# Moving the packs-times-W_in tiles to another place within 256 bytes

## The chip, the core and the metric

The kernel runs on one core of one Trainium2 chip. The metric is the device time of one execution in microseconds (us), taken as the median of several runs. Beside the runs stands one execution recorded by the hardware profiler; all rows shown below come from it.

## The reference

Two attentions in a row, and a feed-forward network behind them, all in float32:

```python
p_packed = sm_attn(p, k, v)              # 32 packed queries per head read all 576 tokens
out = sm_attn(q, p_packed, p_packed)     # 576 tokens read the 32 packed rows
x = out.transpose(0, 2, 1, 3).reshape(B * S, H * D)      # 4608 tokens x 512
h = x @ w_in                             # w_in is 512 x 2048
g = h * (1.0 / (1.0 + np.exp(-h)))
return (g @ w_out).astype(np.float32)    # w_out is 2048 x 512
```

There are 8 batches, 8 heads of 64 elements, 576 tokens and 32 packs in each batch.

## The kernel before

The second attention is a sum over packs, so the kernel never forms x. For each batch it multiplies the 32 packed rows of each head by the part of W_in that belongs to that head (line 310). The result, with two heads in turn for each partition, is the tile that is changed here: for one quarter of the 2048 hidden columns it holds 2 x 512 columns. `Packs.upper` (line 587) copies it from PSUM into `pw_hi`, rounded to the shorter float type (float32r) with which TensorE multiplies, and `Packs.lower` (line 590) writes what the rounding left over into `pw_lo`. The shares of the second attention (the softmax of the tokens over the packs) are split in the same way into `a2_hi` and `a2_lo` (lines 551 and 555).

`h_products` (line 622) then makes h for 288 tokens (half a batch) and 128 hidden columns out of six matmuls: for each of two parities upper x upper, upper x lower, lower x upper. The pack tile is the stationary operand, 128 x 128 of it loaded by one LDWEIGHTS for each matmul, and 288 columns of shares are the moving operand. `h_products` runs 32 times for the first two batches with both halves in one call, and 96 times for the other six, with two blocks of 128 hidden columns in one call: 128 calls of twelve matmuls, 1536 in all.

ScalarE applies the activation, GpSimd makes sums of it, ScalarE and VectorE split the result into `g_hi` and `g_lo` (lines 685 and 689), and line 695 multiplies it by W_out: `g` is stationary, and 256 columns of `wo_hi`, `wo_lo` or of sums of them (`sums_of_w`) are moving. In the first two batches these matmuls have 512 moving columns. A list written out by hand (`ORDER`) fixes the order of all steps. On TensorE a stretch of 12 or 24 matmuls of line 622 is followed by one of 21 or 42 of line 695, and so on, with smaller steps of the attention between them (lines 310, 414 and 433).

The code sets where operands begin within 256 bytes. All large tiles start at a multiple of 256 bytes. The shares begin `AT_A` = 20 floats, 80 bytes, into their tile. A small tile of `AT_G` = 16 floats (64 bytes) is allocated ahead of `gp_main`, so that `g`, `g_hi` and `g_lo` of the later six batches begin at 64. `wo_hi`, `wo_lo`, `sums_of_w` and the pack tiles begin at 0. Rows of all of these step in multiples of 256 bytes. So a stationary block of packs lies (0 - 80) mod 256 = 176 bytes past the place of its moving shares, and a stationary block of `g` lies 64 past that of its moving weights (0 past it in the first two batches).

The pack tiles have two pools: `pw` for all packs of the first two batches and for the first two quarters of the others, `pw_b` for the last two quarters of the others. Each name takes two tiles in turn. `edge` is a pool at the right end of the memory that holds one tile of `EDGE` floats, of which 128 are used (line 423); the tiles right of the middle lie against it.

Of the kernel before, what the change touches and what calls it, by code (L numbers as in the profile page):

```python
# [10 lines left out]
F32R = mybir.dt.float32r  # L11
# [8 lines left out]
P = 128  # L20
# [11 lines left out]
JW = DFF // NJ  # L32
# [93 lines left out]
"""  # L126

TP_BUFS = 4
EDGE = 504
AT_G = 16  # L130
AT_A = 20
A_PART = 320
ON_TOKENS = (0,)
SCALE = 1.0 / math.sqrt(D)
# [6 lines left out]
def packed_attention_ffn(ctx: ExitStack, tc: tile.TileContext, pkT, qT, v, w_in, w_out, out):  # L141
# [17 lines left out]
    pw = ent(tc.tile_pool(name="pw", bufs=2))  # L159
# [35 lines left out]
    made = {}  # L195
# [3 lines left out]
    def in_turn(pool, shape, dtype, name, bufs=2):  # L199
        n = turns[id(pool), name] = turns.get((id(pool), name), -1) + 1  # L200
        return pool.tile(shape, dtype, name=name, tag=f"{name}_{n % bufs}", bufs=1)
# [43 lines left out]
    class Weights:  # L245
# [51 lines left out]
        def upper(self, n):  # L297
            hi, _ = self.both(n)
            nc.scalar.copy(hi, self.raw[n][1].bitcast(F32))
# [15 lines left out]
    class Attention:  # L315
# [106 lines left out]
        def scaled1(self):  # L422
            self.pp = edge.tile([P, EDGE], F32, name="pp")[:, :P]
            nc.vector.tensor_tensor(
                self.pp.rearrange("p (r d) -> p r d", r=2),
                self.ps[:, : 2 * D].rearrange("p (r d) -> p r d", r=2),
                self.rd.rearrange("p (r o) -> p r o", o=1).broadcast_to([P, 2, D]),
                ALU.mult,
            )
# [112 lines left out]
        def upper2(self, hf):  # L542
            if (self.b, hf) == (EARLY - 1, 1):
                both = [a2x.tile([P, 2, A_PART], F32R, name=name) for name in ("a2_hi", "a2_lo")]
            else:
                both = [in_turn(a2p, [P, 2, A_PART], F32R, name, 3) for name in ("a2_hi", "a2_lo")]
            hi, lo = (t[:, :, AT_A : AT_A + HS] for t in both)
            made["a2", self.b, hf] = hi, lo
# [8 lines left out]
    class Packs:  # L557
# [21 lines left out]
        def upper(self):  # L579
            b, j = self.b, self.f // FJ  # L580
            if self.f % FJ == 0:
                pool = pw_b if b >= EARLY and j >= 2 else pw
                both = [in_turn(pool, [P, 2 * JW], F32R, name) for name in ("pw_hi", "pw_lo")]
                made["pw", b, j] = [t.rearrange("p (r n) -> p r n", r=2) for t in both]
            c = slice(self.f % FJ * P, (self.f % FJ + self.nf) * P)
            self.hi, self.lo = (t[:, :, c] for t in made["pw", b, j])
            nc.scalar.copy(self.hi, self.ps)
# [426 lines left out]
```

## Time and profile before

| what | value |
|---|---|
| median of 3 runs | 675.63 us (675.42 to 675.71) |
| the profiled execution's own time | 674.6 us |
| its span, first to last instruction | 672.8 us |
| TensorE busy | 655.4 us, 97% |
| VectorE, ScalarE, GpSimd busy | 66%, 65%, 36% |
| granted TensorE clock | 1.00 of full speed |

The span is what the trace shows; 1.8 us of the profiled execution lie around it. Matmuls are pipelined: the duration of one in the trace is longer than the step from one to the next, so a rate is read from the distance between starts, or from the length of a stretch divided by its number of matmuls.

### The profile page before, as it was taken

Reading aid. Unit: us, or ns where it says so; the run is one execution under the profiler, and the core shown is the slowest. Engines: PE = TensorE matmul, PEld = TensorE weight load, DVE = VectorE, ACT = ScalarE, POOL = GpSimd, SP = SyncE. Lnnn points to the kernel's source line nnn. Section 1 sums busy time; section 2 is a strip of 40 time slices with the busy share of each in tenths; the row PEclk is TensorE's granted clock in tenths of the full one; section 3 lists DMA queues with packets and bytes.
Section 4 is the critical chain, followed back from the end, with each engine's and each line's share of the span. In section 5 each row is a group of like instructions: output and inputs, shape, how many; then the busy total and the mean of one; then the engine's idle time right before and its main releaser. Section 6 shows DMA issues by size and latency. Waiting matters only on the chain.

```text
span 672.8 us, 15186 instructions
## 1 busy us (share of the span) xinstructions
PE 655.4 (97%) x6130; PEld 588.5 (87%) x6130; DVE 442.2 (66%) x618; ACT 435.5 (65%) x732; POOL 245.0 (36%) x361
## 2 busy tenths in 40 slices
PE   8889999999999999999999999999999999999997
PEld 6666787888868989999989999989899999989996
DVE  4999999987755457745675535773748554654375
ACT  4797997764656547654865645676676658646652
POOL 1101214343304434344476343425363343444400
PEclk9999999999999999999999999999999999999999
DMA  9748674858879597785846738783788677470614
GB/s 358 331 158 335 221 270 150 297 208 302 328 293 361 165 374 266 288 276 172 310 158 269 304 84 323 282 348 116 255 321 326 236 240 297 156 284 30 219 48 142
DMA packets 55077, 166.60 MB, mean 248 GB/s; under 512 B 21472, under 2 KB 26592, under 8 KB 47328
## 3 DMA queue, kind: packets, MB, share of 16 engines
q1 hardware_dynamic: 55008, 165.63, 67.1%
q8 instruction: 49, 0.80, 0.5%
q14 instruction: 20, 0.16, 0.1%
HBM read 134.74 MB, written 26.74 MB: 240 GB/s over the span
## 4 chain that ended last, share of the span: by engine, by line
PE 72%; DVE 11%; DMA 6%; ACT 5%; issue 4%; POOL 1%; SPq 1%; DVEq 0%; ACTq 0%; POOLq 0%
PE ps_acc L695 42%; PE ps_two L622 24%; PE ps_two L310 5%; DMA win<-in_w_out 2%; DMA sums_of_w<-sums_of_w 2%; DVE g_lo L689 2%; DVE o L853 1%; ACT g_hi L685 1%; DVE g_lo L640 1%; DMA w_quarter<-w_in 1%; DVE w_raw L279 1%; PE ps_two L414 1%; DVE pw_lo L590 1%; PE ps_two L695 1%; DVE win L291 1%
## 5 line engine op out<-in xcount | busy, mean ns | idle before, releaser
L689 DVE TENSOR_TENSOR g_lo<-g,g_hi 128x896 fp32r<-128x896 f32 x112 | 126.6, 1136 | 121.8 <-ACT g_hi L685 118.5
L695 PE MATMUL ps_acc<-wo_hi,g_hi 128*128 128x256 f32 (+1 forms) x556 | 170.0, 306 | 0.1
L695 PE MATMUL ps_acc<-wo_hi,g_lo 128*128 128x256 f32 (+1 forms) x556 | 169.3, 305 | 0.7 <-DVE g_lo L689 0.4
L695 PE MATMUL ps_acc<-wo_lo,g_hi 128*128 128x256 f32 (+1 forms) x556 | 168.7, 303 | 0.0
L622 PE MATMUL ps_two<-a_hi,pw_hi 128*128 128x288 f32 x512 | 151.8, 296 | 2.9 <-DVE pw_lo L590 1.7
L685 ACT CAST g_hi<-g 128x896 fp32r<-128x896 f32 x112 | 104.3, 935 | 74.5 <-POOL g L657 44.1
L622 PE MATMUL ps_two<-a_lo,pw_hi 128*128 128x288 f32 x512 | 150.8, 295 | 0.2 <-DVE a_lo L555 0.2
L622 PE MATMUL ps_two<-a_hi,pw_lo 128*128 128x288 f32 x512 | 150.8, 294 | 0.0
L655 POOL TENSOR_TENSOR g<-g 128x128 f32<-128x128 f32 x104 | 54.2, 521 | 250.7 <-ACT g L644 243.2
L695 PE MATMUL ps_acc<-sums_of_w,g_hi 128*128 128x256 f32 x632 | 126.3, 281 | 0.2 <-DMA sums_of_w<-sums_of_w 0.2
L695 PEld LDWEIGHTS ps_acc<-wo_hi,g_hi 128*128 128x128 f32 x556 | 104.5, 188 | 8.8 <-issue 4.4
L695 PEld LDWEIGHTS ps_acc<-wo_hi,g_lo 128*128 128x128 f32 x556 | 104.6, 188 | 7.8 <-DVE g_lo L640 2.1
L695 PEld LDWEIGHTS ps_acc<-sums_of_w,g_hi 128*128 128x128 f32 x632 | 96.5, 188 | 14.4 <-issue 10.1
L695 PEld LDWEIGHTS ps_acc<-wo_lo,g_hi 128*128 128x128 f32 x556 | 104.4, 188 | 3.9
L622 PEld LDWEIGHTS ps_two<-a_hi,pw_hi 128*128 128x128 f32 x512 | 96.6, 189 | 9.4 <-DVE pw_lo L590 3.0
L622 PEld LDWEIGHTS ps_two<-a_lo,pw_hi 128*128 128x128 f32 x512 | 96.3, 188 | 1.4 <-DVE a_lo L555 0.6
L622 PEld LDWEIGHTS ps_two<-a_hi,pw_lo 128*128 128x128 f32 x512 | 96.0, 188 | 0.2 <-DVE pw_lo L590 0.2
L695 PE MATMUL ps_acc<-sums_of_w,g_lo 128*128 128x256 f32 x316 | 87.7, 278 | 0.0
L656 POOL TENSOR_TENSOR g<-g 128x256 f32<-128x256 f32 x104 | 81.2, 782 | 6.6
L644 ACT ACTIVATE g<-ps_two 128x512 f32<-128x512 f32 x96 | 56.7, 599 | 40.2 <-PE ps_two L622 20.0
L657 POOL TENSOR_TENSOR g<-g 128x128 f32<-128x128 f32 x104 | 64.2, 618 | 6.6
L695 PEld LDWEIGHTS ps_acc<-sums_of_w,g_lo 128*128 128x128 f32 x316 | 59.4, 188 | 0.2 <-DVE g_lo L689 0.2
(145 smaller groups left out, 893.5 us busy)
## 6 DMA issues: line engine op xcount, KB each, us to landing
sums_of_w<-sums_of_w SPq DMA_DIRECT2D x74, 768.0 KB, 5.8
w_quarter<-w_in SPq DMA_DIRECT2D x22, 1024.0 KB, 8.0
kvq_t<-in_v SPq DMA_DIRECT2D x8, 1280.0 KB, 9.1
kvq_t<-in_pkT SPq DMA_DIRECT2D x7, 1216.0 KB, 8.1
out<-o SPq DMA_DIRECT2D x16, 512.0 KB, 3.1
kvq_t<-in_qT SPq DMA_DIRECT2D x7, 1152.0 KB, 8.4
w_raw<-in_w_in SPq DMA_DIRECT2D x6, 1024.0 KB, 6.9
sums_of_w<-w_sums SPq DMA_DIRECT2D x8, 768.0 KB, 3.7
```

Source lines behind the costliest of these rows:

```text
L279: nc.vector.scalar_tensor_tensor(low, up, -(2**31), low, op0=ALU.bitwise_and, op1=ALU.bitwise_or)
L291: (nc.gpsimd if n in ON_POOL else nc.vector).tensor_tensor(z, z, self.raw[n][0], ALU.add)
L310: nc.tensor.matmul(bank(par)[NP * i : NP * i + NP], lhs(r, i), rhs(r, i), start=True, stop=True)
L414: nc.tensor.matmul(self.ps[NP * i : NP * i + NP, par * D : par * D + D], e, vs[:, c, h * D : h * D + D], start=(c == 0), stop=(c == 4),)
L622: nc.tensor.matmul(bank, p[:, par, cols], a[:, par], start=(n == 0), stop=(n == len(todo) - 1))
L644: nc.scalar.activation(g[:, : 4 * P].rearrange("p (e s) -> p e s", e=2), made["h", u, None][..., :MAIN], AF.Silu)
L655: engine.tensor_tensor(x[:, 4], x[:, 0], x[:, 2], ALU.subtract)
L656: engine.tensor_tensor(x[:, 5:7], x[:, 0:5:4], one, ALU.subtract)
L657: engine.tensor_tensor(x[:, 7], x[:, 3], x[:, 6], ALU.add)
L685: nc.scalar.copy(both[0], g)
L689: nc.vector.tensor_tensor(g_lo, g, g_hi.bitcast(F32), ALU.subtract)
L695: nc.tensor.matmul(out, g[:, rows], w, start=(first and n == 0), stop=(last and n == 2), skip_group_check=True)
```

## The change

`pw_hi` and `pw_lo` become the two halves of one tile, `pw_both`. It has 64 floats more than the two together, and its content begins `AT_PW` = 14 floats (56 bytes) into it. The blocks of packs so begin at 56 within 256 bytes, which is (56 - 80) mod 256 = 232 past the place of the shares. The `edge` tile shrinks from 504 to 184 floats to make room. No instruction is added or removed, and the order stays.

```diff
-EDGE = 504
+EDGE = 184
 AT_G = 16
 AT_A = 20
+AT_PW = 14
...
             if self.f % FJ == 0:
                 pool = pw_b if b >= EARLY and j >= 2 else pw
-                both = [in_turn(pool, [P, 2 * JW], F32R, name) for name in ("pw_hi", "pw_lo")]
-                made["pw", b, j] = [t.rearrange("p (r n) -> p r n", r=2) for t in both]
+                both = in_turn(pool, [P, 4 * JW + 64], F32R, "pw_both")[:, AT_PW : AT_PW + 4 * JW]
+                made["pw", b, j] = both.rearrange("p (n r x) -> n p r x", n=2, r=2)
```

Each of the four tiles grows by 256 bytes, and `edge` gives back 1280. Tiles on the left that come after `pw` move by 512 bytes, those after `pw_b` (`g`, `g_hi`, `g_lo`) by 1024, and those on the right by 1280. All these are multiples of 256, so only the packs change their place within 256 bytes.

## Rows read from the trace of the kernel before

**Rows 1.** The page: span, busy time of TensorE, its granted clock in 40 slices.
```profile
span 672.8 us, 15186 instructions
PE 655.4 (97%) x6130; PEld 588.5 (87%) x6130; DVE 442.2 (66%) x618; ACT 435.5 (65%) x732; POOL 245.0 (36%) x361
...
PEclk9999999999999999999999999999999999999999
```

**Rows 2.** The page: the chain that ended last, shares by engine and line.
```profile
PE 72%; DVE 11%; DMA 6%; ACT 5%; issue 4%; POOL 1%; SPq 1%; DVEq 0%; ACTq 0%; POOLq 0%
PE ps_acc L695 42%; PE ps_two L622 24%; PE ps_two L310 5%; DMA win<-in_w_out 2%; DMA sums_of_w<-sums_of_w 2%; DVE g_lo L689 2%; DVE o L853 1%; ACT g_hi L685 1%; DVE g_lo L640 1%; DMA w_quarter<-w_in 1%; DVE w_raw L279 1%; PE ps_two L414 1%; DVE pw_lo L590 1%; PE ps_two L695 1%; DVE win L291 1%
```

**Rows 3.** Busy time by stretch; first figures: span of stretch, PE, PEld.
```profile
30.00:120.00 90.00, 84.85 (x659) 65.29 (x644) 85.88 (x124) 76.32 (x127) 20.02 (x15) 1.00 0.60 216
...
400.00:500.00 100.00, 99.82 (x1051) 93.28 (x1050) 59.94 (x84) 64.17 (x104) 43.49 (x66) 1.00 0.71 266
```

**Rows 4.** The chain in order of time, 500 to 560: start, length, matmuls.
```profile
507.19 3.16 PE ps_two L622 x24
510.35 2.38 PE ps_acc L695 x21
512.73 1.13 PE ps_two L310 x32
513.86 2.67 PE ps_acc L695 x21
516.53 1.58 PE ps_two L622 x12
518.11 2.38 PE ps_acc L695 x21
...
536.11 1.57 PE ps_two L622 x12
537.68 4.76 PE ps_acc L695 x42
```

**Rows 5.** The same view, 120 to 140, where line 695 has 512 columns.
```profile
127.97 2.73 PE ps_acc L695 x12
```

**Rows 6.** TensorE in order of time behind line 310: start, duration.
```profile
441.36 0.28 PE L695 MATMUL ps_acc<-sums_of_w,g_lo 128*128 128x256 f32 x1
...
442.54 0.28 PE L695 MATMUL ps_acc<-wo_hi,g_hi 128*128 128x256 f32 x1
```

**Rows 7.** The same view where line 695 follows line 622.
```profile
301.60 0.29 PE L622 MATMUL ps_two<-a_lo,pw_hi 128*128 128x288 f32 x1
301.73 0.29 PE L622 MATMUL ps_two<-a_hi,pw_lo 128*128 128x288 f32 x1
301.86 0.39 PE L695 MATMUL ps_acc<-sums_of_w,g_hi 128*128 128x256 f32 x2
```

**Rows 8.** The page: groups of line 622, busy, mean ns, idle before and releaser.
```profile
L622 PE MATMUL ps_two<-a_hi,pw_hi 128*128 128x288 f32 x512 | 151.8, 296 | 2.9 <-DVE pw_lo L590 1.7
...
L622 PEld LDWEIGHTS ps_two<-a_hi,pw_hi 128*128 128x128 f32 x512 | 96.6, 189 | 9.4 <-DVE pw_lo L590 3.0
...
L622 PEld LDWEIGHTS ps_two<-a_hi,pw_lo 128*128 128x128 f32 x512 | 96.0, 188 | 0.2 <-DVE pw_lo L590 0.2
```

**Rows 9.** Line 587 by itself: what its engine waited for (us, times).
```profile
  PE ps_two L310: 16.2, 15
```

**Rows 10.** Durations (min/median/max ns) of the writers that split tiles.
```profile
L587 ACT CAST pw_hi<-ps_two x35: 375/1016/1086, 18.0 to 591.8; 128x1024 fp32r<-128x1024 f32 x31, 128x256 fp32r<-128x256 f32 x4
...
L551 ACT CAST a_hi<-tm x14: 665/675/725, 71.0 to 605.6; 128x576 fp32r<-128x576 f32 x14
```

**Rows 11.** Who waited for whom: TensorE on the pack tiles.
```profile
PEld ps_two L622 <- DVE pw_lo L590: 3.2, 4, 2.3
...
PE ps_two L622 <- DVE pw_lo L590: 1.7, 2, 1.4
```

**Rows 12.** Instructions of line 695 from 205.4 on: stretch, PE busy.
```profile
205.40:673.00 467.60, 286.84 (x2358) 277.20 (x2358) 1.00 0.65 236
```

## The prediction

> **What bounds the kernel now.** I read the page first. TensorE is busy for 655.4 of 672.8 us, at the full clock in every slice, which is the upper of its two levels, 2.4 GHz [rows 1]. The chain that ended last is 72% TensorE; line 695 has 42% of the span, line 622 has 24%, no other line over 5% [rows 2]. Busy time by stretch says where that holds: between 400 and 500 us TensorE is busy 99.8%, in the early part (30 to 120) 94% [rows 3]. So the kernel ends when TensorE has worked through its list, and what counts is the step from one matmul to the next.
>
> That step is read from the chain in order of time, where TensorE's stretches stand with their lengths [rows 4]. Line 622 takes 3.16 us for 24 matmuls, 1.58 or 1.57 us for 12: 131 to 132 ns each, and 131.0 is what I use. At 2.4 GHz 288 columns need 288 / 2.4 = 120 ns, so 11.0 ns of each step is not streaming. Line 695 has two rhythms for the same instruction. Mostly 21 take 2.38 us and 42 take 4.76, 113.3 ns each, which is 6.6 over its 256 / 2.4 = 106.7. Behind line 310 a stretch of 21 takes 2.67 us. That is not the first wait alone: the single starts of such a stretch go from 441.36 to 442.54 in ten steps, 118.0 ns each, 11.3 over [rows 6]. With 512 columns twelve take 2.73 us, 227.5 each, 14.2 over 213.3 [rows 5]. So the excess in the short rhythm is near one sixteenth of the columns (6.6 of 106.7, 14.2 of 213.3); the long rhythm of line 695 adds some 4.5 ns. Line 622 at 11.0 has the excess of the long rhythm, in every stretch of these rows. Its own sixteenth would be 7.5 ns, a step of 127.5.
>
> **The change part by part.** *No instruction comes or goes.* The same 1536 loads and matmuls of line 622 read the packs from another place.
>
> *The new place under the loads.* This is the whole of the possible gain, and the trace of before has no stretch with packs at 56. Bounds of the step: from below 120.0, pure streaming at the granted clock; from above the long rhythm of line 695 carried over, 118.0 / 106.7 x 120 = 132.7. Within these I take the short rhythm, 127.5. The reason: the same kind of instruction is seen in both rhythms at one and the same relation (64 bytes, line 695), the relation of 0 with 512 columns is short too [rows 5], and only the relation of 176 is always long; 232 lies 24 bytes from 0 and 56 from 176. That is nearness, not proof, and it gets less than half the chance. The gain is 3.5 ns x 1536 = 5.4 us of TensorE time.
>
> *What of it reaches the end.* Line 622 takes 131.0 x 1536 = 201 us of TensorE, and the chain holds 24% of 672.8 = 161 us of it [rows 2]: 0.8. In the later stretches TensorE has nearly no idle time [rows 3], which speaks for 1.0. I take 0.9, so 4.8 us.
>
> *One tile in place of two, reading.* If a matmul now waits for the whole tile, the first upper product waits for VectorE's lower part too, which it could have done without for two steps. It does so already: of the time in which a load of line 622 waited for `pw_lo`, 3.0 us stand at the load of `pw_hi` and 0.2 at that of `pw_lo` [rows 8]; all such waits are 3.2 + 1.7 us in six places [rows 11]. Cost 0, at most 6 x 0.26 = 1.6 us if these six had been caused by something else.
>
> *One tile in place of two, writing.* ScalarE's write of the next upper part now has to wait until the old lower part is read as well, one matmul later (0.13 us). Line 587 never waited for matmuls of line 622; all its 16.2 us are for the products of line 310 [rows 9]. Cost 0. What hides it is the slack of the second tile in turn; without that it would be 35 x 0.13 = 4.6 us.
>
> *Writing at 56.* The copies of 1024 elements take 1.02 us at place 0, or 0.99 ns per element; shares, written at 80, take 675 / 576 = 1.17 [rows 10]. If the new place brought line 587 to 1.17, it would be 35 x 0.18 = 6.6 us of ScalarE, off TensorE's path but for the six waits: 6 x 0.18 x 2 = 2.2 us with VectorE's part at most. I take 0, since that row reads from memory and not from PSUM, and its length is fixed cost in part.
>
> *The smaller `edge`* moves the other tiles by multiples of 256 bytes. No instruction depends on it, and the stretches of line 695, which go through several tiles at many distances, show one speed. Cost 0.
>
> Sum: the profiled execution goes from 674.6 (span 672.8 and 1.8 around it) to 669.8. The median of the runs shown is 1.0 us above that execution, so the forecast is 675.6 - 4.8 = 670.8 us.
>
> **A rule of the Trainium skill against it.** The rows show that the last matmul of line 622 in a stretch, under which a block of `g` at 64 is loaded (240 past the shares), takes the same 0.13 us as the one before it, with packs at 176 past [rows 7]. The Trainium skill, SBUF — State Buffer, section "Who interferes with whom", says that TensorE has two independent read ports, one for the moving operand and one for weight loads, and never waits on anyone. By that rule the distance of the two operands cannot matter, and the sum would be 675.6. The two rhythms of line 695 at one relation do not settle it, since their cause is not in the rows.
>
> **The rivals.** *First, nothing changes: 675.6.* The excess of line 622 belongs to the moving shares (at 80) or to the length of 288, not to where the packs lie. For it: rows 7, at 240, eight bytes from the new relation, with no gain. Against it: that is one matmul at a time inside a rhythm set by those before, and a stretch of line 695 does change its step with nothing changed but what ran before.
>
> *Second, slower through the place itself.* All operands of TensorE in the rows begin at multiples of 16 bytes (0, 64, 80); 56 is none. If a load from there takes longer and the step with it, line 622 goes to the upper bound of 132.7: 1.7 x 1536 x 0.9 = 2.4 us, 678.0. It decides from a step of 132.0 on (1.0 x 1536 x 0.9 = 1.4 us, which is 0.2%). For it: no row shows such a place. Against it: a load lasts 188 to 189 ns and overlaps the steps of 131 [rows 8], so a little more need not show. The Trainium skill, SBUF — State Buffer, section "Door 1: The DMA port swizzle", says that the memory's lines are of 16 bytes and that each access that crosses to a new one pays a penalty, which would be 33 lines for 32 here; no run here shows that yet.
>
> *Third, slower through line 695.* Now each stretch of line 695 that follows one of line 622 is short, even where line 695 before it was long: 2.67, then 1.58 of line 622, then 2.38 [rows 4]. So line 622 as it runs now seems to bring the short rhythm back. If its new step hands the long one on instead, most of the short matmuls become long. Of the 2358 from 205 us on [rows 12] about a quarter are long now by the share of stretches behind line 310, so 1770 x 4.5 ns x 0.9 = 7.2 us are lost and 4.8 won: 678.0. It decides from (4.8 + 1.4) / (4.5 ns x 0.9) = 1530 of them on.
>
> *Fourth, far faster.* With no excess at all line 622 saves 11.0 x 1536 x 0.9 = 15.2 us: 660.4. No stretch in the rows is under one sixteenth, so this is unlikely.
>
> **How the numbers follow.** Forecast 0.47, its own range 668 to 673: 0.8 to 1.0 of the gain is 671.3 to 670.2; a step only half way to the short rhythm is 673.2; if the quarter of line 695 that is long turns short as well, it is 588 x 4.5 x 0.9 = 2.4 us less. Nothing changes 0.27. Slower through the place 0.12, slower through line 695 0.10. Far faster 0.04. A measurement of this kernel tells 0.2%, some 1.4 us, from no change. So faster 0.51, same 0.27, slower 0.22. The range from 668.0 to 678.5 leaves out the far gain (0.04), the part of the two slower cases that goes further than priced, with the bounds of reading and writing (0.10), and a rest of the forecast (0.03).
>
> **What would show it.** Right: stretches of 24 in line 622 at 3.06 us, of 12 at 1.53, and line 695 still at 2.38 for 21 behind them. First rival: 3.15 unchanged. Second: 3.18 or more. Third: 3.06 and then 2.47 for 21. If the waits for `pw_lo` grow or line 587 waits for TensorE's matmuls, the single tile is to blame. The prediction is wrong if the step of line 622 does not depend on where the packs lie, or if its rhythm decides that of line 695.

## The result and the profile after

The changed kernel is slower: 679.74 us (median of 6 runs, 679.05 to 680.85) against 675.52 for the kernel before (6 runs, 674.7 to 677.6), a ratio of 1.0063 with a 95% interval of 1.0046 to 1.0081. The forecast was 670.8 with a range up to 678.5.

The page after, same parts as [rows 1, 2] (all line numbers are one higher than before, so 623 is the packs' matmul and 696 that of W_out):

```profile
span 679.1 us, 15186 instructions
...
PE 660.6 (97%) x6130; PEld 592.2 (87%) x6130; DVE 443.3 (65%) x618; ACT 435.2 (64%) x732; POOL 243.5 (36%) x361
...
PEclk9999999999999999999999999999999999999999
...
PE 77%; DVE 10%; DMA 6%; issue 3%; ACT 3%; SPq 1%; POOL 1%; DVEq 0%; ACTq 0%; POOLq 0%
PE ps_acc L696 44%; PE ps_two L623 25%; PE ps_two L311 5%; DMA win<-in_w_out 2%; DMA sums_of_w<-sums_of_w 2%; DVE o L854 1%; DVE g_lo L641 1%; DVE g_lo L690 1%; DMA w_quarter<-w_in 1%; DVE w_raw L280 1%; PE ps_two L415 1%; DVE pw_both L591 1%; DVE win L292 1%; ACT g_hi L686 1%; DMA w_raw<-in_w_out 1%
```

The same instructions at the same clock keep TensorE busy 5.2 us longer, and the chain leans on it more. The profiled execution has a span of 679.1 us, 6.3 more than before. It is the slowest of the six (680.85 us), while the one before lay 1.0 us under its median, so this is more than the 4.2 us between the medians; the sizes below are those of the two profiled executions. Where the 6.3 us lie is seen in the chain in order of time (start, length, matmuls), the stretches that answer to [rows 4] and, in the first two lines, to [rows 5]:

```profile
125.86 1.57 PE ps_two L623 x12
127.44 2.77 PE ps_acc L696 x12
...
420.06 4.95 PE ps_acc L696 x42
...
511.77 3.13 PE ps_two L623 x24
514.90 2.47 PE ps_acc L696 x21
517.37 1.13 PE ps_two L311 x32
518.50 2.59 PE ps_acc L696 x21
521.09 1.57 PE ps_two L623 x12
522.66 2.47 PE ps_acc L696 x21
```

The stretches of the packs, whose place was changed, are as long as before or a hair shorter: 3.13 us for 24 against 3.16, 1.57 for 12 against 1.58. The stretches of W_out behind them, which were not touched, went from 2.38 to 2.47 us for 21, from 4.76 to 4.95 for 42, and with 512 columns from 2.73 to 2.77 for 12. And the roles have changed: before, W_out was long (2.67) behind line 310 and short behind the packs; now it is shorter behind line 311 (2.59, with a first wait in both) and long behind the packs. What ran ahead of line 310 counts there. Taken by the last seven distances inside each stretch of W_out (short under 115 ns, long over it), 32 matmuls of line 310 between two stretches mostly turned the rhythm over: before, 10 of 11 short stretches were followed by a long one and 3 of 3 long by a short one; after, 9 of 10 long by a short one and 4 of 4 short by a long one.

The starts of the matmuls in the trace give the means of the steps (waits, over 145 ns, or 245 with 512 columns, left out, and so is the last stretch of W_out, 237 matmuls): W_out with 256 columns from 114.41 to 116.90 ns over 2121 steps, which is 5.3 us; W_out with 512 columns from 228.47 to 230.87 over 384 matmuls, 0.9 us; the packs from 131.11 to 130.75 over 1536, 0.55 us less. Together 5.6 of the 6.3 us of span.

A list of who waited for whom gives the waits at the pack tile (us in total, times, longest). They are those of [rows 11], to the digit:

```profile
PEld ps_two L623 <- DVE pw_both L591: 3.2, 4, 2.3
PE ps_two L623 <- DVE pw_both L591: 1.7, 2, 1.4
```

Line 588 by itself (durations; then what its engine waited for) still waits for line 311 alone [rows 9] and takes as long [rows 10]:

```profile
L588 ACT CAST pw_both<-ps_two x35: 372/1015/1092, 17.4 to 596.8; 128x1024 fp32r<-128x1024 f32 x31, 128x256 fp32r<-128x256 f32 x4
...
  PE ps_two L311: 16.6, 16
```

### The profile page after: what moved, and what is told of

It reads as the page before. It is cut to its first block, busy times and chain, and to the rows that moved or that the text cites. A ratio compares the mean times of both kernels' runs of the same rounds, so it can differ in the third digit from the quotient of the medians.

```text
span 679.1 us, 15186 instructions
## 1 busy us (share of the span) xinstructions
PE 660.6 (97%) x6130; PEld 592.2 (87%) x6130; DVE 443.3 (65%) x618; ACT 435.2 (64%) x732; POOL 243.5 (36%) x361
## 4 chain that ended last, share of the span: by engine, by line
PE 77%; DVE 10%; DMA 6%; issue 3%; ACT 3%; SPq 1%; POOL 1%; DVEq 0%; ACTq 0%; POOLq 0%
PE ps_acc L696 44%; PE ps_two L623 25%; PE ps_two L311 5%; DMA win<-in_w_out 2%; DMA sums_of_w<-sums_of_w 2%; DVE o L854 1%; DVE g_lo L641 1%; DVE g_lo L690 1%; DMA w_quarter<-w_in 1%; DVE w_raw L280 1%; PE ps_two L415 1%; DVE pw_both L591 1%; DVE win L292 1%; ACT g_hi L686 1%; DMA w_raw<-in_w_out 1%
## 5 line engine op out<-in xcount | busy, mean ns | idle before, releaser
L623 PE MATMUL ps_two<-a_hi,pw_both 128*128 128x288 f32 x1024 | 217.7, 294 | 2.8 <-DVE pw_both L591 1.7
L623 PEld LDWEIGHTS ps_two<-a_hi,pw_both 128*128 128x128 f32 x1024 | 168.6, 188 | 9.5 <-DVE pw_both L591 3.2
L623 PE MATMUL ps_two<-a_lo,pw_both 128*128 128x288 f32 x512 | 150.4, 294 | 0.2 <-DVE a_lo L556 0.2
L696 PE MATMUL ps_acc<-sums_of_w,g_hi 128*128 128x256 f32 x632 | 128.0, 284 | 0.6 <-DMA sums_of_w<-sums_of_w 0.6
L623 PEld LDWEIGHTS ps_two<-a_lo,pw_both 128*128 128x128 f32 x512 | 96.0, 187 | 1.4 <-DVE a_lo L556 0.4
L591 DVE TENSOR_TENSOR pw_both<-ps_two,pw_both 128x1024 fp32r<-128x1024 f32 (+1 forms) x35 | 39.2, 1126 | 16.0 <-ACT pw_both L588 15.8
L649 ACT ACTIVATE rest<-ps_two 128x64 f32<-128x64 f32 x96 | 26.1, 287 | 28.1 <-PE ps_two L623 27.6
```

What stands on the lines that cost most here:

```text
L591: nc.vector.tensor_tensor(self.lo, self.ps, self.hi.bitcast(F32), ALU.subtract)
L623: nc.tensor.matmul(bank, p[:, par, cols], a[:, par], start=(n == 0), stop=(n == len(todo) - 1))
L649: nc.scalar.activation(rest[:, 2 * p : 2 * p + 2, :, b % 2, hf], made["h", u, None][..., MAIN:HS], AF.Silu)
L696: nc.tensor.matmul(out, g[:, rows], w, start=(first and n == 0), stop=(last and n == 2), skip_group_check=True)
```

## The experiments

All kernels are the changed one with what the diff shows. Except for the first, each ran once, beside 1 or 13 runs of the kernel before; ten runs of the first lie between 674.24 and 678.35 us, so single times tell little and the steps in the traces are what is read. A stretch of W_out is called short when its mean step is under 114.2 ns, long when it is over 116.5.

**The place alone, put back.** Is it the place, the single tile, or the other tiles that moved?

```diff
-AT_PW = 14
+AT_PW = 0
```

> The changed kernel with the packs put back to 0 in 256 bytes (176 past the shares); the single tile, the 64 spare floats and the smaller edge stay. Theory H (the hand-over: the step of line 695 is set by what line 622 leaves behind, and that by the place of the packs): as before the change, 675 to 676 us; stretches of 21 of line 695 behind line 623 at 2.38 us. Theory L (the layout: the tiles moved by 1024 and 1280 bytes make line 695 long): 679 to 680 us, 2.47 us for 21. Theory T (the single tile makes someone wait): 679 to 680 us with new waits at the pack tile.

Measured: 675.02 us (median of 10) against 675.49 (13), ratio 1.0 (0.9985 to 1.0015). The chain in order of time:

```profile
506.83 3.16 PE ps_two L623 x24
509.99 2.38 PE ps_acc L696 x21
512.37 1.13 PE ps_two L311 x32
513.50 2.67 PE ps_acc L696 x21
```

These are the lengths of [rows 4] again. The single tile, the smaller `edge` and all tiles moved by it stay in this kernel, so theories L and T fall: within the interval, 1 us either way, the 56 bytes are the whole of the loss.

**Other places.** `AT_PW` = 16, 20, 8, 28, 36 and 52 floats.

> Packs at 64 in 256 bytes, 240 past the shares, a multiple of 16. Theory H gives no sign in advance: a step of the packs' matmul between 126 and 134 ns, and the length of the stretches of W_out behind it either 2.38 or 2.47 us for 21, the time following from both (2.47: 679; 2.38 with 131 ns: 675; 2.38 with 127.5: 670). If only a start off 16 bytes does the harm, 2.38 and at most 675.5. Theory L: 2.47 whatever the place.

> Packs at 80 in 256 bytes, at the same place as the shares (0 past them), the relation at which the 512-column matmuls of the first batches run at 227 ns. Theory H: the step of the packs' matmul near 127.5 ns if that relation carries over; then 670 us with W_out behind it at 2.38 us for 21, 674 with 2.47. Theory L: 2.47 whatever the place.

> Packs at 32 in 256 bytes, 208 past the shares. Theory P (the place sets only the order in which the packs' steps settle, their mean stays at 130.5 to 132 ns, and what the last of them leaves behind sets W_out's step): mean of the packs' steps 130.5 to 132; each stretch of W_out behind them at 113.3 or at 118, all alike or as the one before was; 674 to 680 us. Theory S (some place brings the packs' step itself to one sixteenth over streaming, 127.5 ns): 3 to 5 us less than that at the right place.

> Packs at 112 in 256 bytes, 32 past the shares. Theory P: mean of the packs' steps 130.5 to 132 ns, W_out behind them at 113.3 or 118, 674 to 680 us. Theory S: 127.5 ns at the right place, 3 to 5 us less.

> Packs at 144 in 256 bytes, 64 past the shares, the relation that W_out's matmuls of the later batches have. Theory P: mean of the packs' steps 130.5 to 132 ns, 674 to 680 us. Theory S, for which this is the likeliest place: 127.5 ns in the packs' matmul, 669 to 672 us with W_out at 113.3, 674 to 676 us with 118.

> Packs at 208 in 256 bytes, 128 past the shares, half way round. Theory P: mean of the packs' steps 130.5 to 132 ns, W_out behind them at 113.3 or 118, 674 to 680 us. Theory S: 127.5 ns at the right place, 3 to 5 us less.

Measured, with the two places known already. The steps are means over the starts in the trace; the third column counts the 56 stretches of W_out with 256 columns that come right behind packs (the last one left out), by the nearest whole step (113 to 114 ns, 118 ns; the rest lie between).

| place of the packs, and past the shares | packs' mean step, ns | W_out behind: near 113 or 114 / 118 | us |
|---|---|---|---|
| 0, 176 | 131.1 | 52 / 3 | 675.02 (10 runs) |
| 32, 208 | 130.2 | 0 / 55 | 679.05 |
| 56, 232 (the change) | 130.75 | 1 / 55 | 679.74 (6 runs) |
| 64, 240 | 131.8 | 31 / 25 | 677.73 |
| 80, 0 | 131.9 | 4 / 50 | 680.50 |
| 112, 32 | 131.8 | 48 / 8 | 677.35 |
| 144, 64 | 132.4 | 19 / 37 | 678.91 |
| 208, 128 | 132.5 | 35 / 21 | 678.48 |

Theory S falls: at no place does the packs' step come near 127.5 ns, not even at 144, where its distance is that of W_out in its short rhythm. The packs' mean moves within 130.2 and 132.5. Theory P holds in the main: what differs by place is the order of the single steps, and which rhythm W_out takes behind them. Its band of 130.5 to 132 ns for the packs' mean was missed at 32, 144 and 208. The distances between the starts of one stretch of 24 in each kernel (ns), taken from the traces:

```
before:    130 131 132 130 132 131 131 131 132 130 131 131 132 131 131 131 131 132 130 131 132 131 131 131
place 56:  132 131 134 131 138 126 134 126 134 126 134 126 134 126 134 126 134 126 134 126 134 126 134 127
place 64:  135 128 132 132 135 127 133 131 135 128 132 132 135 128 132 132 135 127 133 131 135 128 132 132
place 80:  134 129 135 130 133 127 129 134 131 132 127 129 134 131 133 126 129 135 130 133 127 129 134 128
```

That is the prediction's excess of 11 ns, spread differently. At 64 the packs only hand on what they were given: behind a stretch of W_out that ended long the next was long in 19 smooth cases of 20, behind one that ended short it was short in 29 of 29 (smooth: no wait within the packs' stretch). At 208 they hand it on too, in 18 of 19 and 30 of 30 (short here: under 114.5). At 144, which theory P did not foresee, they mostly turn it over: behind a short end the next was long in 27 of 27, behind a long end short in 15 of 21. At 0 the next is short and at 32 or 56 long, whatever came before.

**An odd count.** At 56 the steps alternate between 134 and 126, and 12 or 24 end on the lesser one. Leaving out the last product in the second block of each call makes 11 or 22 of them (the output lacks this term):

```diff
             todo = [(p, a, par) for par in range(2) for p, a in ((p_hi, a_hi), (p_hi, a_lo), (p_lo, a_hi))]
+            if at:
+                todo.pop()
```

> The changed kernel with the last of the six products (lower packs times upper shares of the second parity) left out in the second block of each call: stretches of 11 or 22 in place of 12 or 24, so the output lacks that term. In the changed kernel the steps of the packs' matmul alternate between 134 and 126 ns and W_out behind it goes at 118. Theory H in its narrow form (what counts is at which of the two steps the stretch ends): behind 11 the stretch of W_out goes at 113.3, behind 22 at 118. Theory H in its wide form (the place of the packs decides, not the count) and theory L: 118 behind both.

Measured: 666.8 us with 124 matmuls fewer. The chain in order of time, one stretch of 11 and one of 22, each with the W_out behind it:

```profile
510.78 1.44 PE ps_two L625 x11
512.23 2.38 PE ps_acc L698 x21
...
519.16 2.87 PE ps_two L625 x22
522.03 2.48 PE ps_acc L698 x21
```

Over the whole trace: behind 11 smooth steps W_out was short 22 times of 23 and once in between; behind 22, long 20 times of 21. All of these stretches end on the same kind of product, so it is not the operand. Six stretches of 22 hold a wait. In four it fell at the twelfth step, just inside the second call; the ten steps left end on the greater one, and W_out was short in all four, as here (distances in ns, the packs' and then W_out's). In the other two it fell at the first step; they end on the lesser one, and W_out was long in one and had a wait of its own in the other.

```
133 131 134 131 138 126 134 126 134 126 135 237 133 134 131 137 127 133 127 133 127 133
116 114 113 114 113 113 114 113 113 114 113 113 114 113 113 114 113 113 114 113 206
```

**An even count again.** The control for the run before: two products left out, 10 or 20 (the output lacks both terms).

```diff
+            if at:
+                todo = todo[:-2]
```

> The changed kernel with two of the six products (the two with a lower part of the second parity) left out in the second block of each call: stretches of 10 or 20, even again, so the output lacks these terms. If what counts is at which of the two alternating steps a stretch of the packs ends, W_out goes at 118 ns behind both, as in the changed kernel. If leaving out work by itself had made W_out short behind stretches of 11, it is 113.3 here too.

Measured: 658.48 us. Long behind 10 in 22 of 23 smooth cases and behind 20 in 19 of 20:

```profile
503.16 1.31 PE ps_two L625 x10
504.47 2.47 PE ps_acc L698 x21
```

So leaving work out does not shorten W_out's step; with packs at 56, ending on the other one of two alternating steps does. That is the narrow form of theory H.

**The place of g.** Does the distance of `g` from the packs decide at the hand-over?

```diff
-AT_G = 16
+AT_G = 24      # with AT_PW = 8; and AT_G = 30 with AT_PW = 14; and AT_G = 64 with AT_PW = 0
```

> Packs at 32, where their mean step is the least so far (130.0 ns) but all stretches of W_out behind them go at 118, and the values g at 96 in place of 64, so that g lies 64 past the packs as in the kernel before the change. If the distance of g from the packs decides at the hand-over, W_out goes at 113.3 behind the packs, and the time is 673 to 674 us, under both kernels. If the two places count each by itself, W_out stays at 118 or takes some other step: 677 to 680 us.

> The changed kernel (packs at 56) with the values g at 120 in place of 64: 64 past the packs, as before the change. If the distance of g from the packs decides at the hand-over, 113.3 ns in W_out and 674 to 675 us; otherwise 118 or another step, 678 to 681 us.

> Packs and values g both at 0, one tile. W_out's loads then lie 0 past its moving columns, as in the first two batches, where 512 columns go at 227 or 231 ns. If the place of g against the moving columns sets whether two rhythms exist, W_out's steps are others than 113.3 and 118; if not, the same two appear, and behind the packs the one that these hand over. 674 to 681 us.

Measured: 681.75, 683.16 and 684.98 us. The distance alone does not bring the short rhythm back: at 32 with `g` at 96, and at 56 with `g` at 120, `g` lies 64 past the packs as before the change. W_out lost its step of 113.3 altogether: 117 or 119 ns with `g` at 96, 118 to 120 at 120, 119.8 at 0, behind packs and behind anything else. With `g` and packs at 0:

```profile
504.28 3.15 PE ps_two L623 x24
507.43 2.51 PE ps_acc L696 x21
```

The packs' steps are as at the same place before (131.1), and 21 of W_out take 2.51 us, 119.5 each. The early stretches with 512 columns, whose `g` is at 0 in all kernels, stay at 228.5. So whether W_out with 256 columns has a short rhythm depends on where its own loads lie (its moving columns stayed at 0), and among the four places tried only 64 has it. With no short rhythm left, these runs cannot say whether the distance from the packs counts at the hand-over as well.

## Why the prediction was wrong

*What bounds the kernel* was right: TensorE's steps set the time, and they carried the loss to the end.

*The step that failed* is "The new place under the loads", where the packs' matmul was taken to go from 131.0 to 127.5 ns, by nearness to relations at which W_out is short. It measured 130.75, a gain of 0.55 us instead of 5.4, and no place among eight came under 130.2. The sum also held W_out at 2.38 us for 21, with no term for a change of its step; behind the packs it went to 2.47, and there the loss lies. The excess of 11 ns of the packs' step has no short counterpart at any of the eight places, as the long rhythm of W_out has, though both are 11 ns over streaming; the equal numbers had led me to carry one instruction's two rhythms over to another with other columns and another place of its moving operand. For the packs' own step the first rival, that nothing changes, was nearly right. Whether its excess belongs to the shares at 80 or to the length of 288 stays open: no run changed either.

*The third rival* is what happened. I had given it 0.10 and priced it at 678.0: 7.2 us lost in W_out, 4.8 won in the packs. Measured are 5.3 us lost with 256 columns and 0.9 with 512, and 0.55 won. That its 678.0 lies near the measured 679.7 is luck in part: it had put both the loss and the gain too high. The loss is smaller because stretches behind line 310, long before, turned short. Its reading of [rows 4], that the packs brought the short rhythm back, was right, and the odd and even counts show the mechanism for packs at 56: the step on which a stretch of packs ends sets the rhythm of the stretch behind it, which then keeps it until the next wait or the next stretch of another line.

*The second rival* (56 is no multiple of 16) can be left: the loads take 187 to 188 ns against 188 to 189 before, the packs' step at 56 is less than at 64, and W_out is long behind 32 and 80 as well, which are multiples of 16. The Trainium skill's sentence on lines of 16 bytes (SBUF — State Buffer, "Door 1: The DMA port swizzle") shows no cost in this case.

*The costs taken as nothing* (reading and writing one tile, writing at 56, the smaller `edge`) were nothing: the kernel with the single tile, the smaller `edge` and the packs at 0 has a ratio of 1.0, the waits are the same, and line 588 writes at 56 in a median of 1015 ns against 1016 at 0. One bound among them is off: 35 x 0.18 is 6.3 us, not 6.6; the sum did not use it.

*The rule of the Trainium skill* weighed in the prediction (SBUF — State Buffer, "Who interferes with whom": the ports for moving operand and weight loads are independent) was taken to mean that the distance of the two operands cannot matter, and in that reading it does not agree with these runs as far as the step goes. One and the same program but for the place of one stationary operand takes 675.0 or 679.7 us, and W_out's step is 113.3 or 119.8 ns by the place of its loads. The measurement decides; whether the ports have to do with it, no run here shows.

What stays open is what the two rhythms are inside TensorE. The runs show that they exist, that the places of the operands select them, and that they are passed on from stretch to stretch; which memory or queue makes a step 4.4 ns longer, no run here shows. No version that does all the work was clearly faster than the kernel before: at 32, the place where the packs' step is least, W_out is long behind 55 of 56 stretches of packs.

## What to carry to other kernels

When a kernel is bound by back-to-back matmuls, measure the step of every kind of matmul after a change of place, not only that of the one that was moved: here the moved one gained 0.4 ns and its neighbour lost 2.5 in the mean, 4.4 behind the packs. A step that has two values in one trace for one instruction is a warning that it depends on what ran before, and then a change anywhere upstream can select the other value. A gain priced from another instruction's step is a guess until a run has that instruction at that place.

## What the runs showed of the hardware

A rhythm can outlive its cause: at 64 the packs handed on the rhythm of the stretch of W_out before them, in 48 of 49 smooth cases, across 12 or 24 other matmuls, and 32 matmuls of line 310 turned it over in 26 of 28 cases before and after the change. And with packs at 56 the parity of a count of matmuls decides 4.4 ns for each of the 21 or 42 behind them.
